# Keys and values as 64 KB rows in three rooms, and four heads to a bank, in a decode attention block on one core

## The chip, the core and the metric

The kernel runs on one core of a Trainium2 chip. The core has TensorE (PE: matmuls into PSUM, with weight loads shown apart as PEld), VectorE (DVE), ScalarE (ACT), GpSimd (POOL) and SyncE (SP, which issues most transfers here). Transfers between the chip's large memory and the core's working memory SBUF are carried out by 16 DMA engines. The metric is the time of one execution on the device, in microseconds (us).

## The reference

One token for each of two batch rows goes through an adaptive layer norm, an attention over a cache of 4096 keys and values in 32 heads, and a small dense layer with Mish. All is in 32-bit floats. `mod` holds six vectors for each batch row, made from the condition `c`.

```python
mod = (silu(c) @ w_mod).reshape(2, 6, 1, 512)          # sa, ca, ga, sb, cb, gb
h = layernorm(x) * (1 + ca) + sa
q = (h @ wq)                                            # 512 -> 32 heads x 128
scores = einsum("bhqd,bhkd->bhqk", q, k_cache) * 128 ** -0.5
o = einsum("bhqk,bhkd->bhqd", softmax(scores), v_cache)
x = x + ga * (o @ wo)                                   # 32 x 128 -> 512
h = layernorm(x) * (1 + cb) + sb
x = x + gb * (mish(h @ w1 + b1) @ w2)                   # 512 -> 1376 -> 512
```

The two caches are 128 MB each (2 x 32 x 4096 x 128 floats), so nearly all bytes that the kernel reads are keys and values, each read once.

## The kernel before

One head's keys for both batch rows are one tile of 128 partitions with 8192 floats (32 KB) each: 4096 keys over 128 partitions give 32 keys per partition (`NS`), times two batch rows, times 128. Its values are laid out alike. A pool `kvp` (L57) holds four such tiles in turn. SP issues all loads, in the order of the list `stream` (L350 to L354): keys of head h, then the values of the head before it; from head 14 on (`LAG`) the values are two heads behind. With every fourth head comes a 2 MB piece `wqo` with the columns of wq and the rows of wo for four heads (L72). A load is issued by `used` (L358) when the tile that it replaces has been read.

For each head (loop L374 to L390), VectorE multiplies the keys of batch row 0 by the query, which lies in SBUF on all partitions (L245), sums over the 128 elements of each key (L248), and does the same for batch row 1: two products and two sums of 4096 elements. `row_max` (L252) takes the largest score per partition and sends it through TensorE; `soft_max` (L258) of the head before stands between the products and the sums on VectorE, and gives ScalarE the offsets for the exponentials `e` (L269). `totals` and `denominators` (L275, L279) sum the exponentials and take the reciprocal.

`weighted_v` (L287) multiplies the values by the exponentials: 16 matmuls of 512 columns per head, each two instructions, in four strips of the array by turns (partitions 0, 32, 64 and 96 of a PSUM bank `ov`; 8 columns of weights). ScalarE copies the bank out (L301), four matmuls `otp` with the reciprocals as columns add the pieces up (L310), and one matmul adds the head's part of `o @ wo` to the bank `att` (L321). The queries of four heads at a time are made by `project_q` (L218): for each batch row the column of h stands on all 128 weight columns (`hb`), so that the result lies on all partitions, and ScalarE copies it to SBUF (L226).

At the end of the program (L391 to L497), the softmax of head 31 is followed by head 30's values and its output, the copy of `att`, the modulation vectors 3 and 4 (`modulation`, L409), head 31's values (L415), its output (L416 to L422), the second layer norm (`centred`, L435), the dense layer w1 (L447), Mish, w2 (L486) and two output transfers, one on SP's queue and one on ScalarE's (L497).

Of the kernel before, what the change touches and what calls it, by code (L numbers as in the profile page):

```python
# [13 lines left out]
P = 128  # L14
WIDTHS = (384, 384, 352, 256)
CHUNKS = [(g, j) for j in range(3) for g in range(4) if WIDTHS[g] > P * j]


@with_exitstack
def kernel(  # L20
    ctx: ExitStack,
    tc: tile.TileContext,
    kv: bass.AP,
    wqo: bass.AP,
    head: bass.AP,
    mod012: bass.AP,
    tail: list,
    out: bass.AP,
):

    nc = tc.nc
    ctx.enter_context(tc.manual_schedule())
    B = 2
    H = kv.shape[0]  # L40
    DH = 128
    D = 512
    G = D // P
    R = P // G
    NS = kv.shape[3] // (B * DH)
    S = NS * P
    HC = 4
    NJ = 3
    EPS = 1e-5
    SCALE = DH ** -0.5  # L50
    LAG = 14
    NCH = len(CHUNKS)
    BIG = B * NS * DH
# [6 lines left out]
    def big(name):  # L60
        return kvp.tile([P, BIG], F32, tag="kv", name=name)

# [5 lines left out]


    wqo_t, k_t, v_t = {}, {}, {}  # L70

    def load_wqo(c):  # L72
        wqo_t[c] = work.tile([P, 2, G, HC * DH], F32, tag="wqo", name=f"wqo{c}")
        nc.sync.dma_start(out=wqo_t[c].rearrange("p a k n -> p (a k n)"), in_=wqo[c])

    def load_k(h):
        t = big(f"k{h}")
        nc.sync.dma_start(out=t, in_=kv[h, 0])
        k_t[h] = t.rearrange("p (b j d) -> p b j d", b=B, d=DH)

    def load_v(h, cuts):
        t = big(f"v{h}")
        for lo, hi in zip((0,) + cuts, cuts + (BIG,)):
            nc.sync.dma_start(out=t[:, lo:hi], in_=kv[h, 1][:, lo:hi])
        v_t[h] = t.rearrange("p (b j d) -> p b j d", b=B, d=DH)

    first = const.tile([P, head.shape[1]], F32, name="first")
    nc.sync.dma_start(out=first, in_=head)
    cq = first[:, 0:P]
    xq = first[:, P : 2 * P]  # L90
    b1c = first[:, 2 * P : 2 * P + NJ * G * B]
    wm0 = big("wm0")[:, : G * 3 * D]
    nc.sync.dma_start(out=wm0, in_=mod012)
    wm0 = wm0.rearrange("p (k n) -> p k n", k=G)
    load_wqo(0)
    load_k(0)
    load_k(1)
    load_v(0, ())
# [5 lines left out]
    sel = ident.rearrange("p (g r) -> p g r", g=G)[:, :, 0:B]  # L104
    fold = const.tile([P, R], F32, name="fold")
# [10 lines left out]
    scale_row = const.tile([B, P], F32, name="scale_row")  # L116
    nc.vector.memset(scale_row, SCALE)
    eps_t = const.tile([P, 1], F32, name="eps_t")
    nc.vector.memset(eps_t, EPS)

    ct = const.tile([P, G, R], F32, name="ct")
    h2t = const.tile([P, G, R], F32, name="h2t")
    actt = const.tile([P, NCH, R], F32, name="actt")
    hq_pad = const.tile([P, NJ * P], F32, name="hq_pad")
    for t in (ct, h2t, actt, hq_pad):
# [3 lines left out]
    for t in ov:  # L129
        nc.vector.memset(t, 0.0)  # L130


    def centred(src, name, first_sum=None):

# [3 lines left out]
        if first_sum is None:  # L138
            nc.vector.tensor_reduce(out=rs[:, 0:1], in_=src, axis=AX.X, op=ALU.add)
        else:  # L140
            first_sum(rs[:, 0:1])
        mps = small_ps(f"mean_{name}")
        nc.tensor.matmul(mps[:, 0:1], lhsT=mean_w, rhs=rs[:, 0:1], start=True, stop=True)
        nc.vector.tensor_scalar(out=xc, in0=src, scalar1=mps[:, 0:1], scalar2=None, op0=ALU.subtract)
# [4 lines left out]
        nc.tensor.matmul(vps[:, 0:1], lhsT=mean_w, rhs=rs[:, 1:2], start=True, stop=True)  # L149
        return xc, vps[:, 0:1], rs  # L150

    def rstd(var, rs):

# [415 lines left out]
```

## Time and profile before

| | us |
|---|---|
| runs shown | 707.56, 709.99, 710.03 |
| their median | 709.99 |
| span of the profiled execution, first to last instruction | 707.5 |
| VectorE busy in it | 599.0 |
| TensorE matmuls busy in it | 378.7 |
| ScalarE busy in it | 66.4 |

For the profiled execution only the span is given and no time beside it; the span lies 0.1 us below the lowest run and 2.5 us below the median.

How to read the lines that follow. In a group's row stand line, engine, operation, output and inputs with their shapes and the count, then the busy time, the mean duration of one in ns, and the engine's idle time just before with what ended it. A row of the chain of waits or of the timeline begins with start and duration in us. A row of the stretch view has the stretch, its length, the busy time and count of PE, PEld, DVE, ACT and POOL, then the granted clock of TensorE as a share of full speed, the share of the DMA engines' time that was busy, and GB/s. One matmul of 32-bit floats stands as two instructions in these rows. Mean durations of matmuls overlap each other; the time that a batch of them takes is read from the chain.

### The profile page before, as it was taken

To read this page: it belongs to the slowest core of one execution; us is meant where nothing else is said; L and a number is where in the kernel's file an instruction comes from. 1 tells how busy PE (TensorE), PEld (TensorE's weight loads), DVE (VectorE), ACT (ScalarE), POOL (GpSimd) and SP (SyncE) were. 2 spreads that over 40 slices of the span, in tenths; PEclk is the share of its full clock that TensorE was granted. 3 is DMA by queue.
4 is the path that set the end of the run, shared out by engine and by line. 5 is a ranking of instruction groups with operands and counts; after the bars stand their busy time and mean duration, and the time that the engine had idled before them with its cause. 6 is when DMAs were issued, how large, how long until landed. Compare 5 with 4: busy or idle time off the path is not lost.

```text
span 707.5 us, 4712 instructions
## 1 busy us (share of the span) xinstructions
PE 378.7 (54%) x1916; PEld 141.0 (20%) x1916; DVE 599.0 (85%) x332; ACT 66.4 (9%) x255; POOL 2.3 (0%) x17
## 2 busy tenths in 40 slices
PE   4424584554644475414855484543655457445776
PEld 2101131112211122102211131111211122111234
DVE  2599999987999699999999799995999799999511
ACT  1100010000100011000100010000100001000010
POOL 1000000000000000000000000000000000000000
PEclk9856586655856677655755587666855667655676
DMA  9999999999999999999999999999999999999991
GB/s 382 426 437 422 439 435 426 434 428 432 432 431 427 440 429 432 431 432 432 430 433 427 439 427 434 428 430 437 430 434 428 433 426 434 434 429 437 415 423 79
DMA packets 11845, 297.65 MB, mean 421 GB/s; under 512 B 1320, under 2 KB 1456, under 8 KB 1712
## 3 DMA queue, kind: packets, MB, share of 16 engines
q1 hardware_dynamic: 11816, 297.36, 97.9%
q8 instruction: 15, 0.25, 0.1%
q14 instruction: 6, 0.05, 0.0%
q10 hardware_dynamic: 8, 0.00, 0.0%
HBM read 297.35 MB, written 0.00 MB: 420 GB/s over the span
## 4 chain that ended last, share of the span: by engine, by line
DMA 46%; DVE 38%; PE 12%; ACT 1%; another core or an unknown queue 1%; issue 1%; SPq 0%; DVEq 0%; ACTq 0%
DMA k<-in_kv 38%; DVE k L245 19%; DVE s L248 17%; DMA v<-in_kv 8%; PE ov L290 5%; PE qps L222 4%; PE otp L310 1%; PE att L321 1%; PE yps L486 1%; DVE n L262 1%; DVE n L261 1%; PE modps L176 0%; ACT e L269 0%; ACT o L301 0%
## 5 line engine op out<-in xcount | busy, mean ns | idle before, releaser
L245 DVE TENSOR_TENSOR k<-k,q 128x4096 f32<-128x4096 f32 x64 | 282.9, 4421 | 52.0 <-DMA k<-in_kv 52.0
L248 DVE TENSOR_REDUCE s<-k 128x32 f32<-128x4096 f32 x64 | 282.3, 4410 | 1.1
L290 PE MATMUL ov<-v,e 128*8 128x512 f32 x1024 | 167.6, 814 | 49.2 <-DMA v<-in_kv 49.2
L266 PE MATMUL mb<-n,scale_row 2*128 2x2 f32 x64 | 17.9, 347 | 152.0 <-DVE n L262 152.0
L222 PE MATMUL qps<-wqo,hb 128*128 128x512 f32 x128 | 71.7, 723 | 0.8 <-DVE hb L213 0.8
L290 PEld LDWEIGHTS ov<-v,e 128*8 128x8 f32 x1024 | 29.7, 110 | 163.0 <-issue 111.9
L266 PEld LDWEIGHTS mb<-n,scale_row 2*128 2x128 f32 x64 | 15.2, 293 | 171.4 <-DVE n L262 166.6
L310 PE MATMUL otp<-m,o 128*128 128x2 f32 x256 | 33.7, 254 | 22.6 <-ACT o L301 22.1
L321 PE MATMUL att<-wqo,ot 128*2 128x512 f32 x62 | 37.8, 697 | 7.8 <-ACT ot L319 7.8
L310 PEld LDWEIGHTS otp<-m,o 128*128 128x128 f32 x256 | 31.0, 191 | 54.0 <-ACT o L301 52.6
L301 ACT COPY o<-ov 128x512 f32<-128x512 f32 x31 | 18.1, 585 | 225.7 <-PE ov L290 225.7
L256 PE MATMUL mt<-ident,m 128*2 128x128 f32 x64 | 15.0, 324 | 44.8 <-DVE m L254 44.7
L222 PEld LDWEIGHTS qps<-wqo,hb 128*128 128x128 f32 x128 | 29.7, 240 | 36.6 <-issue 35.8
L277 PE MATMUL l<-m,ones 128*128 128x2 f32 x64 | 18.7, 362 | 32.2 <-ACT e L269 32.2
L267 ACT COPY m<-mb 128x2 f32<-128x2 f32 x32 | 5.1, 160 | 262.5 <-PE mb L266 262.5
L277 PEld LDWEIGHTS l<-m,ones 128*128 128x128 f32 x64 | 16.0, 310 | 34.9 <-ACT e L269 34.9
L269 ACT ACTIVATE e<-s,m 128x32 f32<-128x32 f32 x64 | 20.0, 313 | 1.2
L256 PEld LDWEIGHTS mt<-ident,m 128*2 128x2 f32 x64 | 3.0, 82 | 66.3 <-DVE m L254 65.3
L226 ACT COPY q<-qps 128x512 f32<-128x512 f32 x16 | 9.4, 586 | 70.2 <-PE qps L222 70.2
L269 ACT ACTIVATION_READ_ACCUMULATOR e<-s,m 128x1 f32 x64 | 11.9, 186 | 0.0
L411 DVE TENSOR_SCALAR m<-modps 128x128 f32<-128x128 f32 x1 | 0.3, 291 | 13.1 <-PE modps L176 13.1
L261 DVE TENSOR_REDUCE n<-mt 2x1 f32<-2x128 f32 x32 | 8.7, 272 | 1.6 <-PE att L321 1.1
(104 smaller groups left out, 92.7 us busy)
## 6 DMA issues: line engine op xcount, KB each, us to landing
k<-in_kv SPq DMA_DIRECT2D x32, 4096.0 KB, 21.5
v<-in_kv SPq DMA_DIRECT2D x31, 4096.0 KB, 29.8
wqo<-in_wqo SPq DMA_DIRECT2D x8, 2048.0 KB, 21.7
wm<-in_mod SPq DMA_DIRECT2D x1, 3072.0 KB, 10.2
tail<-in_tail SPq DMA_DIRECT2D x1, 2752.0 KB, 21.1
tail<-in_tail SPq DMA_DIRECT2D x1, 2048.0 KB, 25.0
v<-in_kv SPq DMA_DIRECT2D x1, 2048.0 KB
v<-in_kv SPq DMA_DIRECT2D x2, 1024.0 KB, 15.0
```

The costliest lines, as they stand in the source:

```text
L222: nc.tensor.matmul(ps, lhsT=hb[b][:, k, :], rhs=wqo_t[ch][:, 0, k, :], start=(k == 0), stop=(k == G - 1))
L245: nc.vector.tensor_tensor(out=k_t[h][:, b], in0=k_t[h][:, b], in1=qv, op=ALU.mult)
L248: nc.vector.tensor_reduce(out=s_t[h][:, b], in_=k_t[h][:, b], axis=AX.X, op=ALU.add)
L256: nc.tensor.matmul(mps[h], lhsT=m_t[h][:, 0:2], rhs=ident, start=True, stop=True)
L261: nc.vector.tensor_reduce(out=n[:, 0:1], in_=mps[h], axis=AX.X, op=ALU.max, negate=True)
L266: nc.tensor.matmul(bps[:, 0:2], lhsT=scale_row, rhs=n[:, 1:3], start=True, stop=True)
L269: nc.scalar.activation(e_t[h % 3][b][:, :, 4 * b : 4 * b + 4], s_t[h][:, b].rearrange("p (c m) -> p c m", m=4), AF.Exp, bias=m[:, 2 + b : ...
L277: nc.tensor.matmul(lps[h][:, 0:2], lhsT=ones, rhs=m_t[h][:, 4:6], start=True, stop=True)
L290: nc.tensor.matmul(ov[h % 2][R * g : R * g + M, :], lhsT=e_t[h % 3][b][:, c, :], rhs=v_t[h][:, b, 4 * c : 4 * c + 4, :].rearrange("p m d - ...
L301: nc.scalar.copy(o_t[h].rearrange("p m d -> p (m d)"), ov[h % 2])
L310: nc.tensor.matmul(tps[:, 0:2], lhsT=o_t[h][:, m, :], rhs=m_t[h][:, 8 + 2 * m : 10 + 2 * m], start=(m == 0), stop=(m == 3),)
L321: nc.tensor.matmul(att[R * g : R * g + B, :], lhsT=ot, rhs=wqo_t[h // HC][:, 1, h % HC, :], start=(h < G), stop=(h >= H - 1 - G),)
```

## The change

The loads are packed anew. `ROOM` is 64 KB per partition, and three rooms take the place of the four tiles. The keys of a head and the values of an earlier one (`behind`) lie side by side in memory as one row of 64 KB per partition (`pair`) and come by one transfer into one room. Heads 8 and 16 (`ALONE`) come without values, so that the values lag one, then two, then three heads. All of wq (8 MB) comes at the start and all of wo (8 MB) after the last pair; then the values of heads 29 and 30, the modulation weights 3 and 4 with b1, head 31's values in four pieces, w1, the modulation weights 5 and w2 in four pieces. A plan holds for each load the items that must have been used before its room is free.

The queries of all heads are made at the start, in strips (32 weight columns, 4 x 512 columns at once), already scaled. For each four heads two matmuls spread their rows over all partitions into PSUM (`qb`), where VectorE reads them. The product and the sum of a head are now one instruction each, over both batch rows (8192 elements).

The exponentials of four heads stand in four groups of 8 of the 32 weight columns, with zeros beside them, and the values of four heads add up in one PSUM bank. The bank is copied out once, the pieces are added up by four matmuls for the four heads, and the reciprocals are applied afterwards by one product. The part of `o @ wo` is done at the end: 28 heads after head 29's values, three after head 30's, and head 31 last.

Further, c and x come as 16 rows of 128 by ScalarE's queue and are spread by matmuls, and `idle` puts matmuls whose result is not used in front of and behind those of the second layer norm (5, 3 and 7).

In the diff, "..." marks what is left out.

```diff
+KV = B * NS * DH
+ROOM = 2 * KV
+ALONE = (8, 16)
+def behind(h):
+    if h == 0 or h in ALONE:
+        return None
+    return h - 1 - sum(h > a for a in ALONE)
...
-    kvp = ctx.enter_context(tc.tile_pool(name="kvp", bufs=4))
+    rooms = ctx.enter_context(tc.tile_pool(name="rooms", bufs=1))
...
-    def load_k(h):
-        t = big(f"k{h}")
-        nc.sync.dma_start(out=t, in_=kv[h, 0])
...
+    cx = const.tile([16, P], F32, name="cx")
+    nc.scalar.dma_start(out=cx, in_=src["cx"])
...
+    first = room(1, "first")
+    w_t["mod012"] = load(first, 0, src["mod012"]).rearrange("p (k n) -> p k n", k=G)
+    w_t["wq"] = load(room(0, "wq"), 0, src["wq"]).rearrange("p (k n) -> p k n", k=G)
+    k_t[0] = heads(load(first, G * 3 * D, src["single"][0]))
+
+    def load_keys(h, n):
+        t = room(n, f"kv{h}")
+        if h in ALONE:
+            k_t[h] = heads(load(t, 0, src["single"][1 + ALONE.index(h)]))
+            return
+        piece = load(t, 0, src["pair"][h - 1 - sum(h > a for a in ALONE)])
+        k_t[h], v_t[behind(h)] = heads(piece[:, :KV]), heads(piece[:, KV:])
...
+    def load_last(n):
+        t = room(n, "last")
...
+        piece = load(t, 0, src["mod34"])
...
+        for a, z in ((0, 4), (4, 6), (6, 7), (7, 8)):
+            load(t, lo + a * KV // 8, whole[:, a * KV // 8 : z * KV // 8])
...
+    plan, holds = [], {0: [("w", "wq")], 1: [("w", "mod012"), ("k", 0)], 2: []}
+    for h in range(1, H):
+        n = (2, 0, 1)[(h - 1) % 3]
+        plan.append((lambda n=n, h=h: load_keys(h, n), n, list(holds[n])))
+        holds[n] = [("k", h)] + ([] if h in ALONE else [("v", behind(h))])
...
+    def used(*items):
+        done.update(items)
+        while plan and done.issuperset(plan[0][2]):
+            plan.pop(0)[0]()
...
         nc.tensor.matmul(mps[:, 0:1], lhsT=mean_w, rhs=rs[:, 0:1], start=True, stop=True)
+        idle(3, name != "a")
...
         nc.tensor.matmul(vps[:, 0:1], lhsT=mean_w, rhs=rs[:, 1:2], start=True, stop=True)
+        idle(7, name != "a")
...
+    def idle(n, really=True):
+        for _ in range(n if really else 0):
+            nc.tensor.matmul(ov[0][:, 0:P], lhsT=ident, rhs=ones, start=True, stop=True)
...
+    for half in range(2):
+        ps = wide_ps(f"qps{half}")
+        for k in range(G):
+            for g in range(G):
+                c = G * half + g
+                nc.tensor.matmul(
+                    ps[R * g : R * (g + 1)],
+                    lhsT=ht[:, k, :],
+                    rhs=w_t["wq"][:, k, 512 * c : 512 * (c + 1)],
...
+        nc.scalar.activation(q_sb[:, half], ps, AF.Copy, scale=SCALE)
+    qb = psum.tile([P, B, 512], F32, tag="qb", name="qb", bufs=1)
+
+    def queries(c):
+        half, g = divmod(c, G)
         for b in range(B):
...
+            nc.tensor.matmul(
+                qb[:, b],
+                lhsT=row_of[R * g : R * (g + 1), b],
+                rhs=q_sb[R * g : R * (g + 1), half],
...
-        qv = q_t[h // HC, b][:, h % HC, None, :].to_broadcast([P, NS, DH])
-        nc.vector.tensor_tensor(out=k_t[h][:, b], in0=k_t[h][:, b], in1=qv, op=ALU.mult)
-
-    def sums(h, b):
-        nc.vector.tensor_reduce(out=s_t[h][:, b], in_=k_t[h][:, b], axis=AX.X, op=ALU.add)
+    def products(h):
+        qv = qb[:, :, None, (h % 4) * DH : (h % 4 + 1) * DH].to_broadcast([P, B, NS, DH])
+        nc.vector.tensor_tensor(out=k_t[h], in0=k_t[h], in1=qv, op=ALU.mult)
+
+    def scores(h):
+        s_t[h] = work.tile([P, B, NS], F32, tag="s", name=f"s{h}")
+        nc.vector.tensor_reduce(
+            out=s_t[h].rearrange("p b j -> p (b j)"),
+            in_=k_t[h].rearrange("p b j d -> p (b j) d"),
...
+        used(("k", h))
...
+            lo = M * (h % 4) + 4 * b
             nc.scalar.activation(
-                e_t[h % 3][b][:, :, 4 * b : 4 * b + 4],
+                e_t[h % 4][b][:, :, lo : lo + 4],
...
+    def values(h):
+        i = group_of[h]
+        for b in range(B):
+            for c in range(NB):
+                g = c % G
+                nc.tensor.matmul(
+                    ov[i % 2][R * g : R * (g + 1), :],
+                    lhsT=e_t[h % 4][b][:, c, :],
+                    rhs=v_t[h][:, b, 4 * c : 4 * c + 4, :].rearrange("p m d -> p (m d)"),
+                    start=(h == groups[i][0] and b == 0 and c < G),
+                    stop=(h == groups[i][-1] and b == B - 1 and c >= NB - G),
+                )
+        used(("v", h))
+
+    def group_out(i, to):
+        lo, n = B * groups[i][0], B * len(groups[i])
+        o = work.tile([P, 4, DH], F32, tag="o", name=f"o{i}")
...
+            nc.tensor.matmul(
+                tps[:, :n], lhsT=o[:, m, :], rhs=pick[:, m, at : at + n], start=(m == 0), stop=(m == 3)
+            )
+        nc.vector.tensor_tensor(out=to, in0=tps[:, :n], in1=total[i], op=ALU.mult)
...
+    def project(hs):
+        for h in hs:
+            g = h % G
+            nc.tensor.matmul(
+                att[R * g : R * g + B, :],
+                lhsT=ot[:, B * h : B * (h + 1)],
+                rhs=w_t["wo"][:, h, :],
...
     for h in range(H):
+        products(h)
+        if h % 4 == 3 and h + 1 < H:
+            queries(h // 4 + 1)
         if h:
             soft_max(h - 1)
...
+        scores(h)
+        if h and behind(h) is not None:
+            values(behind(h))
+            heads_out(behind(h))
         row_max(h)
     soft_max(H - 1)
...
+    values(H - 3)
+    project(range(H - 4))
+    values(H - 2)
+    heads_out(H - 2)
+    project(range(H - 4, H - 1))
+    totals(len(groups) - 1)
...
     values(H - 1)
-    nc.scalar.copy(ot_last[:, 0:B], head_value(H - 1))
+    group_out(len(groups) - 1, ot_last[:, 0:B])
...
+    idle(5)
...
-    for b, eng in enumerate((nc.sync, nc.scalar)):
-        eng.dma_start(out=out[b, 0].rearrange("(g n) -> g n", n=P), in_=y[b::R, :])
+    for b in range(B):
+        nc.sync.dma_start(out=out[b, 0].rearrange("(g n) -> g n", n=P), in_=y[b::R, :])
```

What moves, on three queues. First the loads that SP issues at the end of the program, one row for each transfer (out, in and the shape in floats). Before:

```order
L78 DMA k_1733<-in_kv 128x8192
L84 DMA v_1751<-in_kv 128x8192
L84 DMA v_1784<-in_kv 128x8192
L335 DMA tail_1802<-in_tail 128x4096
L84 DMA v_1835<-in_kv 128x4096
L84 DMA v_1835<-in_kv 128x2048 x2
L335 DMA tail_1855<-in_tail 128x5504
L335 DMA tail_1855<-in_tail 128x2048
L335 DMA tail_1898<-in_tail 128x3072
L335 DMA tail_1898<-in_tail 128x1536
L335 DMA tail_1898<-in_tail 128x1024
```

Here k_1733 is head 31's keys, v_1784 and v_1835 are the values of heads 30 and 31, tail_1802 the modulation weights 3 and 4, tail_1855 w1 with the modulation weights 5, and tail_1898 w2. After the change:

```order
L67 DMA kv_1201<-in_pair 128x16384
L67 DMA wo<-in_wo 128x16384
L67 DMA two<-in_single 128x8192 x2
L67 DMA last<-in_mod 128x4120
L67 DMA last<-in_single 128x4096
L67 DMA last<-in_single 128x2048
L67 DMA last<-in_single 128x1024 x2
L67 DMA tail<-in_w 128x5504
L123 DMA last<-in_mod 128x2048
L67 DMA tail<-in_w_0 128x3072
L67 DMA tail<-in_w_1 128x1536
```

The pair kv_1201 holds the keys of head 31. Between it and head 31's values, the second to fourth of the rows on `last` after in_mod, now stand 8 MB of wo, the values of heads 29 and 30 (8 MB) and the modulation weights (2 MB); before, the same without wo. What follows head 31's values is the same.

Second, one head's work on VectorE (a row for each instruction, with output, inputs and the output's shape; k and kv are the keys, s the scores, m and n the maxima). Before, head 3 from its first product on:

```order
L245 TENSOR_TENSOR k_223<-k_223,q_0_184 128x4096
L261 TENSOR_REDUCE n_310<-mt_306 2x1
L262 TENSOR_SCALAR n_310<-ident,n_310 2x2
L248 TENSOR_REDUCE s_308<-k_223 128x32
L281 RECIPROCAL m_304<-l_318 128x2
L282 TENSOR_TENSOR m_304<-fold,m_304 128x8
L245 TENSOR_TENSOR k_223<-k_223,q_1_191 128x4096
L248 TENSOR_REDUCE s_308<-k_223 128x32
L254 TENSOR_REDUCE m_369<-s_308 128x2
```

After, the same head:

```order
L310 TENSOR_TENSOR kv_223<-kv_223,qb 128x8192
L331 TENSOR_REDUCE n_298<-mt_293 2x1
L332 TENSOR_SCALAR n_298<-ident,n_298 2x2
L314 TENSOR_REDUCE s_306<-kv_223 128x64
L324 TENSOR_REDUCE m_326<-s_306 128x2
```

Two products and two sums became one of each at double the length, the query comes from `qb` in PSUM, and the two operations on the denominators are gone from the head; their successors (L388 and L379) stand on VectorE once for four heads, behind the sums.

Third, TensorE at the end (two is the room with the values of heads 29 and 30, and the name of the PSUM tile with xps and b1). Before, from head 30's values on:

```order
L290 MATMUL ov_105<-v_1784,e_1_166 8x512 x8
L310 MATMUL otp_1906<-m_1814,o_1902 128x2 x4
L321 MATMUL att<-wqo_1513,ot_1911 2x512
L403 MATMUL xps<-att_sb,fold 32x128 x4
L176 MATMUL modps_1921<-tail_1802,ct 32x256 x16
L290 MATMUL ov_106<-v_1835,e_0_167 8x512 x8
```

After:

```order
L356 MATMUL ov_120<-two,e_1_102 32x512 x8
L400 MATMUL att<-wo,ot 2x512 x28
L356 MATMUL ov_120<-two,e_0_103 32x512 x8
L356 MATMUL ov_120<-two,e_1_104 32x512 x8
L386 MATMUL l_1400<-sums_e,ones 128x6
L376 MATMUL otp_1406<-pick,o_1404 128x6 x4
L400 MATMUL att<-wo,ot 2x512 x3
L386 MATMUL l_1415<-sums_e,ones 128x2
L437 MATMUL two<-last,fold 32x128 x4
L441 MATMUL two<-last,ident 128x24
L230 MATMUL modps_1428<-last,ct 32x256 x16
L356 MATMUL ov_119<-last,e_0_105 32x512 x8
```

Ahead of head 30's values (e_0_103) now stands the projection of 28 heads; the row of four otp's serves three heads, the projection behind it has three heads in place of one, and b1's matmul (L441) has moved here from the start.

More of the change, by code (lines that the diff above doesn't have):

```diff
@@ L87, with load @@
[L87 to L98, printed above, removed]
+    def load(t, lo, ap):
+        piece = t[:, lo : lo + ap.shape[1]]
+        nc.sync.dma_start(out=piece, in_=ap)
+        return piece
@@ new lines, in load_tail @@
+    def load_tail(n):
+        t = room(n, "tail")
+        w_t["w1"] = load(t, 0, src["w1"]).rearrange("p (k n) -> p k n", k=G)
+        nc.sync.dma_start(out=late["mod5"], in_=src["mod5"])
+        w_t["mod5"] = late["mod5"].rearrange("p (k n) -> p k n", k=G)
+        lo = G * F
+        for part in src["w2"]:
+            load(t, lo, part)
+            lo += part.shape[1]
+        w_t["w2"] = t[:, G * F : G * F + NCH * D].rearrange("p (c n) -> p c n", c=NCH)
+    plan, holds = [], {0: [("w", "wq")], 1: [("w", "mod012"), ("k", 0)], 2: []}
@@ L101 @@
+    n = next(r for r in holds if holds[r] is not None)
+    plan.append((lambda n=n: load_tail(n), n, list(holds[n])))
+    done = set()
+    def used(*items):
+        done.update(items)
+        while plan and done.issuperset(plan[0][2]):
+            plan.pop(0)[0]()
     nc.scalar.preload_act_table_set("natural_log_exp_and_others")
@@ L469 @@
         )
-    gps = modulation("5", 1, wm5)
+    gps = modulation("5", 1, w_t["mod5"])
     f = const.tile([P, 3, NJ * G, B], F32, name="f")
```

406 lines of the change are left out of this document (170 added, 236 removed).

## The prediction

> **What bounds the kernel now.** I read the page's slices and queues first, then the stretch view, the groups by line and shape, the chain of waits, and last the timeline of the end.
>
> ```profile
> DMA  9999999999999999999999999999999999999991
> q1 hardware_dynamic: 11816, 297.36, 97.9%
> ```
> ```profile
> 100.00:640.00 540.00, 285.85 (x1350) 101.96 (x1346) 491.56 (x242) 50.13 (x199) 0.00 (x0) 0.67 1.00 431
> 11.50:14.50 3.00, 2.96 (x20) 1.16 (x24) 0.00 (x0) 0.00 (x0) 0.00 (x0) 1.00 0.98 421
> ```
>
> The DMA engines are full in every slice but the last. The load queue q1 works 0.979 x 707.5 = 692.6 us. In the long middle stretch the columns behind the clock say that the DMA share is 1.00 at 431 GB/s, while VectorE (third pair) works 491.56 of 540 us. So the kernel is a gapless stream of loads, followed by what cannot be done before the last values have landed. Only three things can shorten it: fewer bytes, a higher rate, or a shorter end.
>
> ```profile
> 645.22 4.43 DVE k L245
> ...
> 659.06 4.43 DVE s L248
> ...
> 663.78 0.39 PE mt L256 x2
> ...
> 666.76 6.32 PE ov L290 x32
> 673.09 0.59 ACT o L301
> ...
> 673.73 1.07 PE otp L310 x8
> ...
> 675.04 1.34 PE att L321 x2
> ...
> 677.70 2.45 PE modps L176 x32
> 680.14 3.49 PE ov L290 x32
> 683.65 0.38 ACT o L304
> ...
> 685.45 0.47 PE xps L418 x8
> ...
> 686.62 0.60 PE mean_b L143 x2
> ...
> 687.93 0.60 PE var_b L149 x2
> ```
> ```profile
> v<-in_kv SPq DMA_DIRECT2D x2, 1024.0 KB, 15.0
> 663.50 1.28 SPq L84 DMA_DIRECT2D v<-in_kv  x3
> ```
>
> This is the chain at the end. The last keys start at 645.22, their sums end at 663.5, then come the softmax, head 30's values (666.76), its output, the modulation, and head 31's values, done at 683.65. The last piece of those values was issued near 664.4 (third of three issues that take 1.28 us from 663.50) and lands 15.0 us later, near 679.4. So here the end does not wait for DMA: the late keys hold it, 4.2 us behind the last values. Behind 683.65 stands a serial stretch of 707.5 - 683.65 = 23.85 us.
>
> **The change, part by part. Stream.** Bytes: the 140 KB of `head` become 8 KB, everything else is loaded once as before: -0.13 MB, at 431 GB/s -0.3 us. Rows double from 32 to 64 KB. The profile has no 64 KB rows. In the stretch from 11.5 us the queue carries `wqo`, rows of 16 KB: 421 / 0.98 = 430 GB/s, against 431 with 32 KB rows. So half as many rows bought 0.3% there, and the next halving buys half of that, 0.15% of 692.6 us: I take -1.0 us, with 0 and -2 as bounds, and -1.3 with the bytes. That longer rows lose is not excluded by any row; it is a rival. The last values then land at 679.4 - 1.3 = 678.1: behind them come the same w1, mod5 and w2, 128 x 13184 x 4 bytes = 6.75 MB, 15.7 us.
>
> **VectorE must stay hidden for that.**
>
> ```profile
> L245 DVE TENSOR_TENSOR k<-k,q 128x4096 f32<-128x4096 f32 x64 | 282.9, 4421 | 52.0 <-DMA k<-in_kv 52.0
> L248 DVE TENSOR_REDUCE s<-k 128x32 f32<-128x4096 f32 x64 | 282.3, 4410 | 1.1
> L261 DVE TENSOR_REDUCE n<-mt 2x1 f32<-2x128 f32 x32 | 8.7, 272 | 1.6 <-PE att L321 1.1 <-PE mt L256 0.5
> L254 DVE TENSOR_REDUCE m<-s 128x2 f32<-128x64 f32 x32 | 7.0, 220 | 1.1
> L262 DVE TENSOR_SCALAR n<-ident,n 2x2 f32<-2x2 f32 x32 | 6.9, 216 | 1.1
> L213 DVE COPY hb<-hps 128x512 f32<-128x512 f32 x1 | 0.7, 691 | 0.5 <-PE hps L168 0.5
> L305 DVE COPY o<-ov 128x256 f32<-128x256 f32 x1 | 0.4, 424 | 3.5 <-ACT o L304 3.5
> L430 DVE TENSOR_TENSOR xg<-xps,mod 128x128 f32<-128x128 f32 x1 | 0.3, 290 | 1.5 <-PE xps L418 1.5
> L436 DVE TENSOR_TENSOR m<-xc_b,m 128x128 f32<-128x128 f32 x1 | 0.3, 288 | 0.0
> ```
>
> A head costs 2 x 4.42 + 2 x 4.41 + 0.27 + 0.22 + 0.22 = 18.4 us, and the two small operations for its denominators are now done once per four heads. The two copies from PSUM give 691 - 424 = 267 ns per 256 elements, so some 0.16 us is fixed, and one long operation in place of two saves it: 18.1 us. A product that reads its queries from PSUM: the product with xps (PSUM) takes 290 ns, the one without takes 288, so at most 2 ns per 128 elements, 0.13 us per head; the dearest case is in the rivals. A pair of 8.39 MB lands every 8.39 / 0.431 = 19.5 us, so 1.3 us per head are spare. At heads 8 and 16 a single lands after 9.7 us; VectorE falls 8.4 us behind and makes it up in seven heads. A room is freed at most 18.1 + 8.4 us after its landing, and the queue holds up to 39 us of other loads then: no gap. The start is hidden too: wq lands near 2 + (3.15 + 8.39) / 0.431 = 29 us, its 64 instructions (0.11 to 0.21 each, by the clock) and the spreading take some 12, and head 0 starts near 42, with two pairs queued.
>
> A pair's keys wait for its values as well, up to 9.7 us longer than alone, with the softmax of the head before queued behind that product; the stream doesn't care, since the rooms above hold.
>
> **Edits off the path.**
>
> ```profile
> L222 PE MATMUL qps<-wqo,hb 128*128 128x512 f32 x128 | 71.7, 723 | 0.8 <-DVE hb L213 0.8
> 704.38 0.65 SPq L497 DMA_DIRECT2D out<-y  x1
> 704.38 1.36 ACTq L497 DMA_DIRECT2D out<-y  x1
> ```
>
> The queries' 128 matmul instructions become 64 in strips, at the start, and 32 that spread their rows; the copies of ov drop to a quarter. The full stream covers all of these, and without that cover they would gain, not lose. The second output DMA moves from ScalarE's queue, where its issue takes 1.36 us, to SP behind the first: 2 x 0.65 = 1.30, so 0.
>
> **Keys leave the end.** Behind the last pair stand wo, two singles, mod34 and the last values, 23.1 MB or 53.6 us: head 31's keys land at 624.5 instead of 645.2, and are done by 643. The old chain through 663.5 is gone. What is late next is TensorE.
>
> ```profile
> L290 PE MATMUL ov<-v,e 128*8 128x512 f32 x1024 | 167.6, 814 | 49.2 <-DMA v<-in_kv 49.2
> L321 PE MATMUL att<-wqo,ot 128*2 128x512 f32 x62 | 37.8, 697 | 7.8 <-ACT ot L319 7.8
> L447 PEld LDWEIGHTS w1ps<-tail,h2t 128*32 128x32 f32 x32 | 2.5, 163 | 2.0 <-issue 1.1 <-DVE h2t L441 0.4
> L290 PEld LDWEIGHTS ov<-v,e 128*8 128x8 f32 x1024 | 29.7, 110 | 163.0 <-issue 111.9 <-DMA v<-in_kv 50.9
> ```
>
> Values 29 land at 653.8 and 30 at 663.5. Head 29's values on a cold array take 6.3 us (the row at 666.76): 660.1. Then 28 heads are projected at once, 56 instructions. They are of the values' form (512 columns into one of four strips), whose 32 take 3.49 us: 0.109 each, 6.1 us, to 666.2. The other bound is a lone pair, 1.34 / 2 = 0.67 each, 37.5 us; I take the first, since consecutive heads go to different strips. Head 30's values: 669.7. This frees the room of the tail, 7 us before the stream gets there. Then comes the stretch that took 673.09 to 683.65 before, 10.56 us of nearly the same instructions, plus 0.3 for b1's matmul: head 31's values are done at 680.6, 3.05 us earlier. Wider weights (32 columns, 163 ns against 110) can add 32 x 0.05 = 1.7 us per head where they aren't covered; I take 0, since busy matmuls cover them in the rows of w1.
>
> **Dummies and the clock.**
>
> ```profile
> 685.90:696.00 10.10, 6.80 (x38) 3.99 (x38) 2.44 (x12) 0.87 (x3) 0.00 (x0) 0.50 0.72 296
> 690.90:696.40 5.50, 5.29 (x32) 2.49 (x32) 0.01 (x1) 0.05 (x1) 0.00 (x0) 0.53 0.39 161
> L168 PE MATMUL h2ps<-ident,hq 128*128 128x8 f32 x2 | 0.6, 370 | 1.5 <-DVE hq L439 1.5
> ```
>
> From 685.9 to 696.0 the granted clock is 0.50. W1's matmuls fill the second stretch: 5.29 us at a mean clock of 0.53. At 1.00 that is 2.8: -2.5. Three lone matmuls go from 0.60 to 0.39 (mt at 663.78): -0.6. The price: a dummy is two instructions with 128-wide weights, like otp's, 1.07 / 8 = 0.134 each, 0.27 per dummy. Five in a gap of 0.7 us (685.92 to 686.62) delay by 0.65, three in 0.7 by 0.1, seven in 1.5 (h2ps waits so long for hq) by 0.4: +1.15. Queued behind them are mean, variance and h2's matmuls, which everything awaits. Net -1.95 us.
>
> [...]
>
> **Sum**: 707.5 - 3.05 - 1.95 = **702.5** by the profiled execution's span. The runs shown lie at 707.56, 709.99 and 710.03, the lowest right on this span, the median 2.5 above. I add 0.5 us for that: **703.0 us**.
>
> **The rivals.**
> (a) The dummies miss: the clock is still 0.50. Then w1 stays at 5.3 and each dummy takes 0.60: +2.3, +1.1 and +2.7 in the three gaps, 707.5 - 3.05 + 6.1 = 710.5. For it: such stretches are cold today. Against: 15 dummies fill the gaps densely. With half the loss, 707.
> (b) VectorE becomes the bound: a read of PSUM, beside TensorE's writes to other banks, slows the long product. It decides from 1.3 us per head (15% of the product). At double the time a head takes 26.8 us, the keys end at 42 + 32 x 26.8 = 900; their room then takes mod34 and the last values (2 + 14.6 us), and 21.9 us of the serial stretch follow: 939 us. With +2 us a head, the keys end at 685 and all at 724. Against it: 290 and 288 ns.
> (c) The projection does not overlap: 37.5 instead of 6.1 us, head 30's values end at 701, and 10.9 + 21.9 us follow: 734 us.
> (d) Rows 64 KB apart move slower. 16 to 32 KB shows none of it; 3% would cost 20 us: 722.
> (e) The change doesn't do what it says: the queue cuts the rows to 32 KB (1 us lost), and TensorE is late by its weights (twice 1.7 us at the end): 704 to 707.
> (f) What halves the clock is not the gaps: w1 stays at 5.3, and the dummies only cost their 1.15: 705.6.
>
> **How the numbers follow.** Forecast 0.66, (a) 0.11, (b), (c) and (d) 0.04 each, (e) 0.07, (f) 0.04. The range 699 to 709.5 holds the forecast with its bounds (below: 1 us more by the rows, and 3 by a clock that is full at heads 29 and 31 and at w2 too; above: 2.5 by the runs' spread), (e), (f) and most of (a). A change of 0.5%, 3.5 us, is about what a measurement here can tell from none. Faster: forecast, (f) and most of (e): 0.76. Same: (a) and the rest of (e): 0.14. Slower: (b), (c) and most of (d): 0.10.
>
> **What would show it.** Right: DMA share 1.00 at 431 to 433 GB/s to about 690; VectorE waiting about 1 us per head for pairs; the last keys' sums done near 643; values 31 done near 681; a clock near 1.00 at w1. Wrong: gaps in the DMA row before the tail, a product over 10 us, w1 still at 5 us, or values 31 waiting for the projection.

## The result and the profile after

| | before | after |
|---|---|---|
| median of five runs each, us | 707.56 (704.67 to 710.03) | 702.17 (699.77 to 702.93) |
| ratio of the times, 95% interval | | 0.991 (0.9881 to 0.9939) |
| profiled execution: span, us | 707.5 | 701.2 (its time is 702.93) |
| VectorE busy, us | 599.0 | 585.7 |
| TensorE matmuls busy, us | 378.7 | 289.7 |

The change makes the kernel 0.9% faster, 5.4 us by the medians and 6.3 us by the two profiled spans. Three of the five runs of before are those shown ahead of the prediction; the other two, 706.95 and 704.67, lie lower, so the median does too. The first lines are from the page of the changed kernel: the DMA row of the 40 slices and the load queue (packets, MB, share of the 16 engines' span).

```profile
DMA  9999999999999999999999999999999999999993
q1 hardware_dynamic: 6928, 297.23, 98.3%
```

The stream is still without a gap, and its work fell from 692.6 us to 0.983 x 701.2 = 689.3 us. The next rows are groups by line and shape (mean ns of one behind the busy time, then the engine's idle time before them).

```profile
L310 DVE TENSOR_TENSOR kv<-kv,qb 128x8192 f32<-128x8192 f32 x31 | 269.2, 8684 | 24.6 <-DMA kv<-in_pair 24.5
L314 DVE TENSOR_REDUCE s<-kv 128x64 f32<-128x8192 f32 x31 | 268.7, 8667 | 0.0
```

The product now reads its queries from PSUM and takes 8684 ns. Two products from SBUF took 2 x 4421 = 8842 ns; a fixed part of some 160 ns in each is an estimate from the two copies of before (2 x 424 - 691 = 157 ns), and one of them less makes 8682. The sums, which read no PSUM, fell alike, from 2 x 4410 = 8820 to 8667 ns. So the PSUM operand costs nothing that these rows can show. VectorE still waits for the pairs, 24.5 us in 31 heads, so it is hidden. TensorE's busy time fell by 89 us (the queries made at once, the projection in strips, one set of otp's for four heads). Most of that lies under the full stream, where the chain of waits gives no sign that it bought time; it was not tested by itself. The chain of waits of the changed kernel at its end (start, duration, what):

```profile
622.27 30.61 DMA two<-in_single
...
652.93 5.17 PE ov L356 x32
...
658.10 6.01 PE att L400 x56
664.11 3.49 PE ov L356 x32
667.62 0.59 ACT o L369
...
669.57 1.80 PE att L400 x6
...
673.24 3.51 PE modps L230 x32
676.75 3.49 PE ov L356 x32
...
680.26 0.38 ACT o L371
...
682.48 1.58 PE ov L247 x10
684.06 0.22 PE mean_b L198 x2
684.28 1.49 PE ov L247 x6
685.77 0.22 PE var_b L205 x2
685.99 2.11 PE ov L247 x14
688.10 0.14 PE h2ps L223 x2
...
688.49 2.83 PE w1ps L477 x16
...
694.38 2.64 PE yps L517 x88
```

VectorE is gone from the end. The chain enters it by the landing of head 29's values (652.93), and from there TensorE is the bound: head 29's values, the projection of 28 heads, head 30's values, its output, the modulation, head 31's values (done at 680.26). Behind that stands the serial stretch of 701.2 - 680.26 = 20.9 us, 23.85 before. The rows `ov L247` are the dummies. The granted clock (first number of the last three) in four stretches, the projection with head 30's values, the modulation, the middle of the dummies, and w1:

```profile
656.00:669.50 13.50, 12.92 (x118) 3.92 (x110) 0.34 (x2) 0.59 (x1) 0.00 (x0) 1.00 0.98 417
669.70:676.60 6.90, 6.74 (x54) 2.82 (x52) 0.17 (x1) 0.59 (x1) 0.00 (x0) 0.51 1.05 436
683.40:686.70 3.30, 3.30 (x18) 3.30 (x17) 1.06 (x6) 0.61 (x3) 0.00 (x0) 0.50 1.00 413
688.40:691.40 3.00, 2.77 (x32) 1.55 (x32) 0.03 (x1) 0.01 (x1) 0.00 (x0) 1.00 0.59 233
```

At w1 (fourth row) the clock is 1.00 where it was 0.53. Before that it was not all good: the modulation ran at 0.51, and among the dummies the clock stood at 0.50 for 3.3 us.

### The profile page after: what moved, and what is told of

Its sections match the earlier page's. It is cut to its first block, busy times and chain, and to the rows that moved or that the text cites. A ratio compares the mean times of both kernels' runs of the same rounds, so it can differ in the third digit from the quotient of the medians.

```text
span 701.2 us, 4047 instructions
## 1 busy us (share of the span) xinstructions
PE 289.7 (41%) x1686; PEld 100.7 (14%) x1686; DVE 585.7 (84%) x224; ACT 39.1 (6%) x185; POOL 3.8 (1%) x19
## 3 DMA queue, kind: packets, MB, share of 16 engines
q1 hardware_dynamic: 6928, 297.23, 98.3%
HBM read 297.23 MB, written 0.00 MB: 424 GB/s over the span
## 4 chain that ended last, share of the span: by engine, by line
DVE 47%; DMA 44%; PE 7%; issue 0%; ACT 0%; another core or an unknown queue 0%; SPq 0%; DVEq 0%; ACTq 0%
DMA kv<-in_pair 34%; DVE kv L310 22%; DVE s L314 22%; DMA first<-in_single 6%; DMA two<-in_single 4%; PE ov L356 3%; DVE first L310 1%; PE att L400 1%; PE ov L247 1%; PE modps L230 1%; DVE n L332 1%; DVE n L331 1%; PE otp L376 0%; PE w1ps L477 0%; PE yps L517 0%
## 5 line engine op out<-in xcount | busy, mean ns | idle before, releaser
L310 DVE TENSOR_TENSOR kv<-kv,qb 128x8192 f32<-128x8192 f32 x31 | 269.2, 8684 | 24.6 <-DMA kv<-in_pair 24.5
L314 DVE TENSOR_REDUCE s<-kv 128x64 f32<-128x8192 f32 x31 | 268.7, 8667 | 0.0
L356 PE MATMUL ov<-kv,e 128*32 128x512 f32 x928 | 169.2, 896 | 5.2 <-ACT e L340 5.2
L336 PE MATMUL mb<-n,ones 2*128 2x2 f32 x64 | 17.9, 347 | 225.6 <-DVE n L332 225.6
L295 PE MATMUL qb<-q_sb,row_of 32*128 32x512 f32 x32 | 28.4, 1035 | 64.2 <-DVE kv L310 64.2
L356 PEld LDWEIGHTS ov<-kv,e 128*32 128x32 f32 x928 | 37.2, 157 | 119.4 <-issue 110.4
L336 PEld LDWEIGHTS mb<-n,ones 2*128 2x128 f32 x64 | 16.1, 307 | 234.5 <-issue 157.5
L388 DVE RECIPROCAL total<-l 128x8 f32<-128x8 f32 (+2 forms) x9 | 1.7, 185 | 26.9 <-PE l L386 26.9
L295 PEld LDWEIGHTS qb<-q_sb,row_of 32*128 32x128 f32 x32 | 8.8, 302 | 72.3 <-DVE kv L310 66.4
L282 PE MATMUL qps<-wq,ht 128*32 128x512 f32 x64 | 9.2, 737 | 13.9 <-DMA wq<-in_wq 13.9
L376 PE MATMUL otp<-pick,o 128*128 128x8 f32 (+2 forms) x72 | 9.5, 258 | 3.7 <-ACT o L369 3.2
```

What stands on the lines that cost most here:

```text
L282: nc.tensor.matmul(ps[R * g : R * (g + 1)], lhsT=ht[:, k, :], rhs=w_t["wq"][:, k, 512 * c : 512 * (c + 1)], start=(k == 0), stop=(k == G - 1),
L295: nc.tensor.matmul(qb[:, b], lhsT=row_of[R * g : R * (g + 1), b], rhs=q_sb[R * g : R * (g + 1), half], start=True, stop=True,)
L310: nc.vector.tensor_tensor(out=k_t[h], in0=k_t[h], in1=qv, op=ALU.mult)
L314: nc.vector.tensor_reduce(out=s_t[h].rearrange("p b j -> p (b j)"), in_=k_t[h].rearrange("p b j d -> p (b j) d"), axis=AX.X, op=ALU.add,)
L336: nc.tensor.matmul(bps[:, 0:2], lhsT=ones[0:B, :], rhs=n[:, 1:3], start=True, stop=True)
L356: nc.tensor.matmul(ov[i % 2][R * g : R * (g + 1), :], lhsT=e_t[h % 4][b][:, c, :], rhs=v_t[h][:, b, 4 * c : 4 * c + 4, :].rearrange("p m d ...
```

## The experiments

Three theories stood beside each other for the 6 us: the rows of 64 KB (the stream), the order (keys away from the end), and the dummies (the clock). Each was taken out of the changed kernel or put alone into the one before. Ratios are to the kernel before on the same chip, with 95% intervals.

**The changed kernel again**, as the yardstick for what follows.

> The changed kernel once more, as the measure for the three beside it. Every theory: 702 us, 0.9% under the kernel before, values 31 done near 680.3 in the span, w1 near 2.8 us, w2 near 2.6 us.

701.54 us (701.20 to 702.21), 0.9915 (0.9887 to 0.9944); the kernel before had 707.68. Its chain differs from the one above mainly at the dummies:

```profile
680.01 0.38 ACT o L371
...
682.23 1.31 PE ov L247 x10
...
683.66 0.78 PE ov L247 x6
...
684.76 1.67 PE ov L247 x14
```

The same 15 dummies take 3.76 us here, 0.24 to 0.26 each, and 5.18 us above. The granted clock over them:

```profile
682.20:686.50 4.30, 4.30 (x40) 4.12 (x36) 2.27 (x11) 0.87 (x3) 0.00 (x0) 1.00 1.01 419
```

It is 1.00 throughout here and was 0.50 for 3.3 us above, in two executions of the same program. The spans differ by 701.2 - 699.6 = 1.6 us, the dummies by 1.4.

**No dummies.**

```diff
     def idle(n, really=True):
-        for _ in range(n if really else 0):
+        for _ in range(0):
```

> The changed kernel without its 15 unused matmuls. Theory 1 (they hold the clock): the gaps shrink by 2.25 us in all, but the three lone matmuls go back from 0.22 to 0.60 us, w1 from 2.8 to 5.3 and w2 from 2.6 to 4.3: +3.1 us, 705 us, granted clock near 0.5 at w1. Theory 2 (what halves the clock is not the short gaps): w1 stays near 2.8 and the 2.25 us are won, 700 us. Theory 3 (the whole gain is the stream's): no change, 702.

703.66 us (701.37 to 704.74), 0.9945 (0.9921 to 0.9969): the dummies are worth 703.66 - 701.54 = 2.1 us by the medians. The intervals overlap, and the lowest run without them lies within the range of the yardstick. The traces bear the size out: behind head 31's values (done at 681.28 here) 21.6 us follow, 19.6 in the repeated run. Its chain, and the clock from the gaps into w1:

```profile
685.35 0.52 PE var_b L205 x2
...
687.39 0.61 PE h2ps L223 x2
...
688.25 4.82 PE w1ps L477 x16
...
696.12 2.64 PE yps L517 x88
```
```profile
685.60:692.00 6.40, 4.61 (x31) 3.01 (x33) 1.05 (x5) 0.87 (x3) 0.00 (x0) 0.50 0.73 296
```

W1 takes 4.82 instead of 2.83 us. W2 (yps) takes 2.64 us with and without them: in this execution that part of the shorter end is not their doing.

**Nine dummies in place of 15.**

```diff
-        idle(3, name != "a")
+        idle(2, name != "a")
...
-        idle(7, name != "a")
+        idle(5, name != "a")
...
-    idle(5)
+    idle(2)
```

> 2, 2 and 5 unused matmuls instead of 5, 3 and 7. Each takes 0.16 us per instruction, 0.32 in all; the three gaps are 0.7, 0.7 and 1.5 us without any. Theory 1: they then fill the gaps and delay nearly nothing, -1.5 us if the clock stays at 1.00 (700.5 us); if the clock falls to 0.50 on the way, w1 is back near 5 us and the sum is +1 to +3. Theory 2: -1.9 us whatever their number.

703.47 us (700.11 to 704.58), 0.9932 (0.9909 to 0.9955): no better than none at all, though the interval reaches the one of 15. Its w1, and the clock ahead of it:

```profile
687.46 4.27 PE w1ps L477 x16
```
```profile
683.60:690.00 6.40, 6.14 (x36) 4.81 (x37) 1.61 (x9) 0.87 (x3) 0.00 (x0) 0.50 0.95 390
```

W1 was still at 4.27 us. With nine dummies the clock stands at 0.50 for 6.4 us, as with none, and is back only within w1; with 15 it was at 0.50 for 3.3 us in one execution and not at all in the other. So 15 dummies do not keep the clock from falling, but in both it is back ahead of w1.

**Dummies alone, in the kernel before**, at the same three places.

```diff
+    def idle(n, really=True):
...
+        idle(3, name != "a")
...
+        idle(7, name != "a")
...
+    idle(5)
```

> The kernel before with the same 5, 3 and 7 unused matmuls in the same three places and nothing else. Theory 1 (they are worth about 3 us by themselves, by the clock): w1 from 5.3 to 2.8 us, w2 from 4.3 to about 2.6, gaps +2.25: -2 to -3 us against the kernel before, ratio 0.996. Theory 2 (the clock is kept by something else in the changed kernel): +2.25 us, ratio 1.003.

703.95 us against 708.5, 0.9938 (0.9915 to 0.996): -4.5 us by the medians, more than the 2 to 3 expected. The chain, and the clock from the first dummy to w1:

```profile
683.77 0.38 ACT o L310
...
690.76 2.83 PE w1ps L454 x16
...
696.60 2.64 PE yps L493 x88
```
```profile
685.90:690.70 4.80, 4.54 (x40) 4.24 (x36) 2.42 (x12) 0.87 (x3) 0.00 (x0) 1.00 1.01 418
```

Head 31's values are done at 683.77 as before (683.65), so all of it lies in the serial stretch, which is 703.1 - 683.77 = 19.3 us long. W1 (2.83 in place of 5.29 us) and w2 (2.64 in place of 4.31) came as expected. The surplus lies ahead of them: the expectation charged the dummies 2.25 us, as measured in the first execution of the changed kernel, but here the clock is 1.00 and the three gaps grew by only 0.8 us (0.70, 0.71 and 1.52 us without dummies became 1.31, 0.78 and 1.67). W2's own loss in the kernel before goes with this fall of the clock:

```profile
699.30:702.80 3.50, 3.47 (x69) 3.50 (x73) 0.00 (x0) 0.00 (x0) 0.00 (x0) 0.53 0.02 5
```

Between w1 and w2 (696.1 to 699.2) it had been back at 1.00. What made it fall again there is not known.

**Rows of 32 KB.** The pair comes as two transfers into the same room; all else stays.

```diff
-        piece = load(t, 0, src["pair"][h - 1 - sum(h > a for a in ALONE)])
-        k_t[h], v_t[behind(h)] = heads(piece[:, :KV]), heads(piece[:, KV:])
+        both = src["pair"][h - 1 - sum(h > a for a in ALONE)]
+        k_t[h] = heads(load(t, 0, both[:, :KV]))
+        v_t[behind(h)] = heads(load(t, KV, both[:, KV:]))
```

> The changed kernel with each pair loaded by two transfers of 32 KB rows (keys, then values) into the same room; the order of the bytes in the stream, the rooms and everything behind them are the same. Theory 1 (the row length makes the stream 2 us shorter): the last values land about 2 us later, near 679.4, head 29's values too, and all that hangs on them: +2 us, 704. Rival (row length does nothing, the stream is shorter by its order, the start or fewer transfers): the last values land at 677.4 as now and the time is 702.

704.36 us (701.54 to 704.69), 0.9949 (0.9932 to 0.9966), 2.8 us above the changed kernel. From its page and its chain:

```profile
q1 hardware_dynamic: 11104, 297.23, 98.5%
```
```profile
681.94 0.38 ACT o L372
```

The same bytes in 11104 packets are 0.985 x 702.5 = 692.0 us of queue work, against 689.3, and head 31's values are done at 681.94 in place of 680.01 to 680.26. The eight traces with the long rows (the changed kernel, its repeated run and its other variants) give 688.8 to 690.0 us of queue work, so the 692.0 stands apart. At head 31's values the run is 1.9 us behind the repeated run; most of the rest of the 2.8 us is the dummies, which took 5.17 us in this execution and 3.76 there. So the long rows are worth 2 to 3 us, 0.4% of the stream, where I had taken 1.0. The edit doubles the number of the pairs' transfers too; whether their number or the rows' length counts was not separated.

**The order alone, in the kernel before**: values three heads behind from head 24, so that head 31's keys come 4 MB earlier and values 29 to 31 last.

```diff
-    behind = {h: h - 1 if h <= LAG - 1 else h - 2 for h in range(1, H) if h != LAG}
+    behind = {h: h - 1 - (h > LAG) - (h > 24) for h in range(1, H) if h not in (LAG, 24)}
...
-    stream += [("v", H - 2), ("w", 0), ("v", H - 1), ("w", 1), ("w", 2)]
+    stream += [("v", H - 3), ("v", H - 2), ("w", 0), ("v", H - 1), ("w", 1), ("w", 2)]
...
+    values(H - 3)
+    head_out(H - 3)
     values(H - 2)
```

> The kernel before with values three heads behind from head 24 on, so that head 31's keys stand 4.2 MB further from the end; rooms, rows and the products stay. Theory 1 (the late keys held the end): the keys' sums end 9.7 us earlier, near 654, head 30's values wait for their landing near 665 instead, and head 31's values are done about 2 us earlier: ratio 0.997. Rival (the last values' landing or the serial stretch alone set the end): no change, ratio 1.000.

722.97 us, 1.0218 (1.0187 to 1.0248): slower. The edit had broken something else, as SP's waits show (total, times, longest):

```profile
SPq L74 <- PE att L321: 67.1, 4, 33.5
```

Head h's part of `wo` lies in the same piece as `wq`, and only two pieces fit; with the longer lag a piece is held longer, and SP waited 33.5 us for it with all later loads behind it. The DMA stood still for one slice. So this run says nothing of the order, but it says why the change took `wq` and `wo` apart. With a third piece the same edit was run again. This line comes on top; the two edits that make room for it, by letting two small tiles of the end share space, are left out here:

```diff
-        wqo_t[c] = work.tile([P, 2, G, HC * DH], F32, tag="wqo", name=f"wqo{c}")
+        wqo_t[c] = work.tile([P, 2, G, HC * DH], F32, tag="wqo", name=f"wqo{c}", bufs=3)
```

> The lag of three heads in the kernel before once more, now with a third tile for the pieces of wq and wo (two small tiles share their room with others for it), since the first try's stream stood still behind such a piece, which waited 33.5 us for a projection. Theory 1 (late keys held the end): no gap in the DMA row, the keys' sums end near 654, head 30's values start at their landing near 665, head 31's values are done near 681.5 instead of 683.65: -2 us, ratio 0.997. Rival (the keys' place does nothing): 683.65 as before, ratio 1.000.

706.11 us against 707.72, 0.9967 (0.9954 to 0.9981): -1.6 us. Its chain:

```profile
645.10 5.94 PE ov L290 x32
...
658.00 6.28 PE ov L290 x32
...
667.61 4.83 PE ov L290 x27
...
681.80 0.38 ACT o L304
```

Head 31's values are done at 681.80, 1.85 us earlier than before. From 645.10 on the chain runs along TensorE's queue, through three heads' values, with head 31's softmax between the first two; the clock is 0.57 in the second row and 0.73 in the third.

**Does the projection overlap?** Consecutive heads go to different strips; here all heads of one strip come one after the other.

```diff
-    project(range(H - 4))
+    project([h for g in range(G) for h in range(g, H - 4, G)])
```

> The changed kernel with the 28 heads projected in the order 0, 4, 8, ... 24, 1, 5, ..., so that consecutive ones use the same strip of the array; nothing is left out. Theory 1 (strips overlap four deep, 0.107 us per instruction): without overlap 56 x 0.43 = 24 us instead of 6.0, head 30's values end 18 us later, near 686, the tail is requested after the stream has run dry (gap of some 10 us in the DMA row), and the time is near 720 us. Rival (the strips do not matter for two columns of weights): 702 us.

714.57 us (a single run). The chain:

```profile
657.95 17.60 PE att L400 x53
...
693.21 0.38 ACT o L371
```

An instruction takes 17.60 / 53 = 0.33 us in place of 6.01 / 56 = 0.107, both at a granted clock of 1.00; head 31's values are done 13.2 us later than in the repeated run, and the time is 13.0 us longer. That the four strips work at once is shown; the price was less than the 720 expected.

**What bounds it next.** The modulation stands in TensorE's queue between heads 30 and 31; moved in front of head 30's output it fills that wait.

```diff
     values(H - 2)
+    mps34 = modulation("3", 2, w_t["mod34"])
     heads_out(H - 2)
...
-    mps34 = modulation("3", 2, w_t["mod34"])
```

> The changed kernel with the modulation 3 and 4 right behind head 30's values instead of ahead of head 31's values. Its weights land at 667.5 and head 30's values end at 667.6. Theory 1 (TensorE's queue, not the last landing, sets when head 31's values are done): the modulation takes about 1.8 us at the full clock instead of 3.5 and partly fills ScalarE's copy; head 31's values are done near 678.3, right behind their last landing at 677.4: -2 us, 700. Rival (the end hangs on the stream alone): no change.

700.02 us (699.64 to 700.98), 0.9887 (0.9862 to 0.9911). The chain:

```profile
643.01 34.02 DMA last<-in_single
...
677.08 1.08 PE ov L356 x4
...
678.18 0.38 ACT o L371
```

The modulation takes 1.90 us here, at a clock of 1.00, in place of 3.51 at 0.51. Now the last piece of head 31's values is waited for; it lands at 677.0. If that is the bound, less work on TensorE must bring nothing more. The next kernel adds to this one that eight heads are projected ahead of head 29's values:

```diff
+    project(range(8))
     values(H - 3)
-    project(range(H - 4))
+    project(range(8, H - 4))
```

> As the run with the early modulation, and 8 of the 28 heads projected ahead of head 29's values, where TensorE waits for their landing anyway. Theory 1: head 30's values start at their landing (662.6) instead of 664.1; but then the last landing (677.4) binds, so -2 us against the changed kernel, as with the early modulation alone, and no more. If more comes, the landing was not the next bound.

700.68 us (699.17 to 701.24), 0.989 (0.9865 to 0.9915): nothing more, as expected.

Then the landing itself was moved: the modulation's weights are loaded behind head 31's values, the modulation takes the place of the first five dummies, and b1's matmul stands ahead of w1.

```diff
-        piece = load(t, 0, src["mod34"])
...
+        piece = load(t, 0, src["mod34"])
...
         late["mod5"] = t[:, lo : lo + G * D]
...
-    nc.tensor.matmul(fps, lhsT=ident, rhs=late["b1"], start=True, stop=False, skip_group_check=True)
-    mps34 = modulation("3", 2, w_t["mod34"])
...
-    idle(5)
-
+    mps34 = modulation("3", 2, w_t["mod34"])
...
+    nc.tensor.matmul(fps, lhsT=ident, rhs=late["b1"], start=True, stop=False, skip_group_check=True)
```

> The changed kernel with the modulation weights 3 and 4 loaded behind head 31's values instead of ahead of them, the modulation and b1's matmul behind head 31's output (in place of the first five unused matmuls). Theory 1: the last values land 4.9 us earlier, near 672.5, TensorE's queue binds (values 31 done near 676.3 instead of 680), the stretch behind costs about the same, and the end comes near the stream's own: -3 us against the changed kernel, 698.5 us, ratio 0.987. Rival (the stretch behind the values is held by the stream's end, 692.7): less than 1 us.

699.22 us (699.15 to 699.39), 0.9873 (0.9857 to 0.9888), the lowest median here. The chain ends:

```profile
641.48 29.17 DMA last<-in_single
...
670.67 22.04 DMA tail<-in_w
...
692.75 0.47 PE yps L515 x8
```

The end now waits for the last transfer of `tail`, w2's: the stream is the bound to its end, and the runs lie within 0.24 us. The clock is 1.00 from 673.4 us on (its mean from 670.67 to 692.75 is 0.94), with ten dummies and the modulation. Only fewer bytes, a faster stream, or less behind its last byte could still shorten this kernel.

## Why the prediction was right, step by step

The forecast was 703.0 us (span 702.5), the result 702.17 (span of the profiled execution 701.2). Two small misses cancel: the span came out 1.3 us below the sum, and the runs lie 1.7 to 1.9 us above their spans (702.93 to 701.2), where I had added 0.5. Also the profiled execution of before was a rather long one: runs of that kernel lie as far above their spans (709.86 to 708.1), so its median of 707.56 is a span of some 705.8. Of the change itself 5.0 us were forecast (707.5 to 702.5) and 5.4 came by the medians.

- **Stream.** Mechanism right, size wrong: -3.3 us of queue work against the -1.3 forecast. The step "the next halving buys half of that, 0.15%", extrapolated from one 3 us stretch of 16 KB rows, was mis-sized: its share of 0.98 is rounded, so 421 / 0.98 lies anywhere from 427 to 432 GB/s, and that stretch could not show 0.3%. The 32 KB run puts the long rows at 2.7 us of queue work and 1.9 to 2.8 us of time, against my bound of 2. The last piece of head 31's values was forecast to land at 678.1 and lands at 677.0 (chain with the early modulation). Rival (d), slower rows, falls, and so does the first half of (e), rows cut to 32 KB: the queue carries 6928 packets, and 11104 where the rows are 32 KB.
- **VectorE hidden.** Right. The last keys' sums end at 641.6, forecast by 643; this row of the timeline of the changed kernel shows the maximum behind them:

```profile
641.59 0.22 DVE L324 TENSOR_REDUCE m<-s 128x2 f32<-128x64 f32 x1
```

  Rival (b), the PSUM operand as a price, falls with 8684 ns. A product from queries copied to SBUF was not tried; by the sums, which fell by 153 ns where the products fell by 158, there is no difference for it to win.
- **Keys leave the end, TensorE is next.** Right, nearly on the spot by errors that cancel. Head 29's values end at 658.10 (660.1 forecast), the projection takes 6.01 us (6.1), head 30's values end at 667.6 (669.7): 2 us ahead, half from the landing (652.93, 653.8 forecast), half from the clock (head 29's values took 5.17 us at a mean of 0.70, and the row of before at 666.76 has 6.32 at 0.57). The stretch to head 31's values then takes 12.64 us, not 10.9: the modulation 3.51 in place of 2.45 and the three heads' projection 1.80 in place of 1.34, at a clock of 0.51, and b1's matmul 0.55, not 0.3. End: 680.26, forecast 680.6. The step that I costed by "nearly the same instructions" kept the instructions but not the clock they ran at. Rival (c) falls by the strip run, which also gives its true price: +13 us, not +31. The wider weights cost nothing: head 30's values take 3.49 us, as head 31's did before with narrow ones; so the second half of (e) falls too.
- **Dummies.** Sign right, and the net size near by pieces that were off. The stretch behind head 31's values became 2.9 us shorter in the first execution (23.85 to 20.94, 1.95 forecast); taking the dummies out costs 2.1. The gaps cost 0.88 + 0.78 + 0.59 = 2.25 us there (1.15 forecast): the gaps of 0.70 and 0.71 us in the chain of before, and of 1.52 us in that of the run without dummies (685.87 to 687.39), became 1.58, 1.49 and 2.11. A dummy was put at 0.27 us, as at a full clock; with the clock at 0.50 for part of this stretch it took 0.30 to 0.50. In the repeated run, at 1.00, it took no more than 0.26. Lone matmuls won 1.2 (0.6 forecast), w1 2.5 as forecast, and w2 1.7, which I had left as it was. In the changed kernel w2's gain is there without dummies too, and w1 without them takes 4.82 us, not 5.29. These two, 1.7 and 0.5 us, are most of what separates the 4.5 us that the dummies bring in the kernel before from the 2.1 in the changed one, as far as one profiled execution of each stands for the others.
- **Rivals (a) and (f).** W1 takes 2.83 us in all seven traces with 15 dummies, at a clock of 1.00 in the first execution; with ten and the modulation in place of five the clock is 1.00 too. With nine and none w1 takes 4.27 and 4.82 us, at 0.66 and 0.58. So the dummies are what gives w1 the full clock, and both rivals fall as told; but (a) held for 3.3 us of the first execution, in which the clock stood at 0.50 among the dummies. What makes the clock fall was not shown. In the first execution of the changed kernel it goes from 1.00 to 0.51 near 669.7, and this is the stretch from the end of head 30's values to there.

```profile
667.60:669.70 2.10, 1.45 (x13) 1.24 (x16) 0.36 (x2) 0.59 (x1) 0.00 (x0) 1.00 1.00 417
```

  TensorE is busy for 1.45 of these 2.10 us, and idle for 0.40 us at most at a time (the timeline ahead of 668.26). Whether the clock falls for the gaps, for the thinness of the matmuls between them or for something else stays open, and so does why it falls among the dummies in one execution and not in the other.

Added up, with the changed kernel at 701.54: rows 2.8 us (0.9 of it behind head 31's values, mostly the clock at the dummies), dummies 2.1 us, which leaves 1.2 of the 6.1 for the order and for whatever else was not taken out by itself; alone in the kernel before, the order gave 1.6 and the dummies 4.5. So the parts do not add exactly. The last sums moved 22 us away from the end (663.5 to 641.6), and that bought under 2, since TensorE's own queue and the last landing stood just behind.

## What to carry to other kernels

When a late wait is taken away, walk the chain again with the next engine in its place and with the clock that it will have there; the gain is the distance to the next bound, not the length of what was removed (here the sums moved 22 us and bought under 2). Where a stream bounds the kernel, length of rows is worth a test of its own (2 to 3 us here), and what little the end computes should be ordered so that the last transfer, not an engine's queue, ends it. What the 15 dummies cost here went with the clock (3.76 us at 1.00, 5.18 with 3.3 us at 0.50), so their number is worth a test: 15 helped here (w1 2.83 us) and nine did not (4.27). Useful matmuls can take the place of some, as the modulation does in the fastest kernel here (699.22 us).

## What the hardware showed that was not expected

- Rows of 64 KB instead of 32 KB, with one transfer in place of two for each pair, moved the same 297.23 MB in 689.3 instead of 692.0 us.
- The clock fell from 1.00 to 0.51 behind 2.10 us in which TensorE was busy for 1.45 us and idle for at most 0.40 us at a time, and stayed there while it was busy for 6.74 of 6.90 us.
- The same 15 unused matmuls took 3.76 us in one execution and 5.18 in another, at a clock of 1.00 and with 3.3 us at 0.50.
- Matmul instructions of 512 columns in one strip of the array, one behind the other, took 0.33 us each; in four strips by turns 0.107 us, a third.
